# Heads 4 to 7 of the first batch through block transposes and transposing DMAs, a smaller scale for q, and weights asked for later

## The chip, the cores and the metric

The kernel runs on one core of one Trainium2 chip. The metric is the device time of one execution in microseconds, taken as the median of several runs. Before the change it is 331.51 us (three runs, 330.75 to 333.87). TensorE is called PE below, VectorE DVE, ScalarE ACT, GpSimd POOL; SP is the engine that issues most of the DMAs.

## The reference

Attention in which a query sees only the keys of its own hash bucket, followed by a feed-forward layer with a layer norm and a residual. Four batches, eight heads, 768 tokens, head width 64, six hash bits, model width 512, hidden width 2048, all in float32:

```python
q_bits = (q @ proj > 0);  k_bits = (k @ proj > 0)          # 6 bits for each token and head
mask = bucket(q_bits) == bucket(k_bits)
scores = where(mask, q @ k.T / 8, -1e9)
attn = softmax(scores) @ v                                  # for each batch and head
x = heads side by side                                      # (4, 768, 512)
out = x + relu(norm(x) * g_ln @ w_ch1) @ w_ch2
```

## The kernel before

**The mask as a matmul.** For each head the kernel keeps q and k transposed, features on partitions 0 to 63, and beside them, on partitions 64 to 69, the six hash bits as plus or minus 24 (`BIT`). One matmul over 70 partitions then gives the score plus 576 for each bit that agrees and minus 576 for each that does not. The exponential (line 373) subtracts the sum for six agreeing bits, so that every other bucket comes out as zero. These operands lie in `slots`, one buffer for even and one for odd batches.

**Two ways to make the operands.** For batch 0 all eight heads go through PE (`head`, line 572): `transposes` turns q and k of one head with six float32 transposes, the results are copied out of PSUM by DVE (q) and ACT (k), and `casts` narrows them into `slots` on POOL and DVE or ACT. `hash_pair` multiplies two heads by `proj` (sixteen float32 passes in the trace), DVE takes the signs (line 300), and four DVE instructions multiply by 48 and write the bits into `slots` (line 306). For batches 1 to 3 the work is taken from PE in another manner: POOL narrows q and k to bfloat16 (`narrow`), a transposing DMA writes `slots` (`operands`, line 253) and a plain DMA moves the odd token tiles down from partitions 64 to 127 (line 256); DVE transposes 32x32 blocks of the float32 tile (`blocks`, line 239), PE multiplies these by a block-diagonal `proj` (`hashes`, line 265), DVE takes signs and scales (lines 273 and 276), and the bits go to DRAM (line 278) and come back into `slots` by four DMAs, one for a head, in rows of 64 bytes (line 280).

**Order of the first stage.** The kernel works in twelve chunks of 256 query tokens, three for each batch. A chunk has four pairs of heads and three units in each pair. A unit is four score matmuls (line 367), one exponential over 128 x 1024 (line 373) and eight value matmuls (line 395). The first two chunks are interleaved by hand in `first_two` (line 577): 24 units in the order pair 0 of chunk 0, pair 0 of chunk 1, pair 1 of both, pairs 2 and 3 of chunk 0, pairs 2 and 3 of chunk 1. The table `also` says what else is emitted in the step of each unit, and each engine keeps that order. In step i the scores of unit i + 1 are emitted first, then the entries of `also[i]`, then the values of unit i. Heads 4 and 5 (pair 2) are first needed by unit 12, heads 6 and 7 by unit 15. Before the change, `head(4)` to `head(7)` stand in steps 5 to 11 and their bits in steps 8 and 12; the layer norm of chunk 0 stands in step 18, and the first two of its eight up-projections (line 455) in steps 22 and 23. From chunk 2 on, a planner mixes the units with the feed-forward work by costs.

**DMA queues.** SP and ACT issue plain DMAs, each on a queue of its own (q1 and q10 in the profile). The weights are cast from float32 to bfloat16 on the way, and POOL issues those DMAs on a third queue (q0): `load_w1` (line 492) straight after `values(0)`, `load_w2` (line 500) in step 7. Each SP or ACT DMA takes the next of eight semaphores and waits at issue for the DMA that used it last. The inputs of batch 1 (`nxt.load(0)`) are asked for at the start, `nxt.load(1)` and `nxt.load_v(0)` in step 9.

Of the kernel before, what the change touches and what calls it, by code (L numbers as in the profile page):

```python
# [16 lines left out]

BIT = 24.0
LBIT = BIT * BIT

# [6 lines left out]
def kernel(  # L27
# [11 lines left out]
    nc = tc.nc  # L39
# [49 lines left out]
    HS = HC * P  # L89
    CMAP = [[2 * i + par for par in range(2) for i in range(HC)]] + [list(range(NC))] * (B - 1)  # L90
    slots = [
# [41 lines left out]
    def load_half(b, half):  # L133

        first = b == 0
        h0 = half * H // 2
        t = {}
        for nm in "qk":
            t[nm] = nat.tile([P, H // 2, NC, D], F32, tag=f"{nm}nat", name=f"{nm}nat")
        cuts = [0, 1, 2, 4] if first and half == 0 else [0, 2, 4]  # L140
        for lo, hi in zip(cuts, cuts[1:]):
            for nm, src, eng in (
                ("q", q, nc.sync), ("k", k, nc.scalar if first else nc.sync)
            ):
                eng.dma_start(
                    out=t[nm][:, lo:hi],
                    in_=src[b, h0 + lo : h0 + hi].rearrange("h (p c) d -> p h c d", p=P),
                )
            if first and half == 0 and lo == 1:
                for i in range(2):  # L150
                    nc.scalar.dma_start(
                        out=proj1[i * D : (i + 1) * D, i, 0:n_bits], in_=proj
                    )

                nc.scalar.activation(wake2[:, 0:1], wake2[:, 1:2], AF.Exp)
                t["v"] = load_values(b, half)
        return t
# [15 lines left out]
    class Prep:  # L173
# [28 lines left out]
        def transposes(self, h, a):  # L202

            if a == 0:
                self.qkT[h] = work.tile([P, 2, HS], F32, tag="qkT", bufs=4, name="qkT")
            if h == 1:
                tp = ps_sc.tile([P, 2, 512], F32, tag="sc", name="tpose")[:, 0, 0:HS]
            else:
                tp = ps_mm.tile([P, HS], F32, tag="mm", name="tpose")
            for i in range(HC):  # L210
                nc.tensor.transpose(  # L211
                    tp[:, i * P : (i + 1) * P],
                    self.tiles[h // 4]["qk"[a]][:, h % 4, 2 * i : 2 * i + 2].rearrange(
                        "p c d -> p (c d)"
                    ),
                    identf,
                )
            evac(self.qkT[h][:, a, :], tp)

# [8 lines left out]
        def narrow(self, half, a):  # L228

            if a == 0:  # L230
                self.nat16[half] = work.tile(
                    [P, H // 2, 2, NC, D], BF16, tag="nat16", bufs=1, name="nat16"
                )
            nc.gpsimd.tensor_copy(self.nat16[half][:, :, a], self.tiles[half]["qk"[a]])  # L234

# [10 lines left out]

        def operands(self, half):


            dst = self.sl[:, half * H // 2 : (half + 1) * H // 2].rearrange(  # L250
                "p h a (i two t) -> p (h a i) two t", two=2, t=P
            )
            nc.sync.dma_start_transpose(
                out=dst[:, :, 0, :], in_=self.nat16[half].rearrange("p h a c d -> p (h a c d)")
            )
            nc.sync.dma_start(out=dst[0:D, :, 1, :], in_=dst[D:P, :, 0, :])

        def hashes(self, half):
# [16 lines left out]
            )  # L275
            nc.vector.tensor_scalar_mul(bits, bits, 2.0 * BIT)
            bd = bounce.tile([P, 2 * NT_], BF16, tag="bits", name="bits_d")
# [11 lines left out]
        def hash_pair(self, j):  # L289
# [14 lines left out]
            for g in range(4):  # L304
                par = g % 2
                nc.vector.tensor_scalar_mul(  # L306
                    self.sl[D:K1, 2 * j + g // 2, :, par * HS : (par + 1) * HS],
                    bits[32 * g : 32 * g + n_bits],
                    2.0 * BIT,
                )  # L310

# [13 lines left out]
        def part(self, kind, half):  # L325

            if kind == "T":
                return [(0, lambda: self.operands(half))]
            if kind == "H":
# [19 lines left out]
    def att_units(b, t, x):  # L349

        sl, va, vs = slots[b % 2], vaug[b % 2], vsum[b % 2]
        units = []
        q0 = t * CT
        for j in range(NP):
# [7 lines left out]
            for g, grp in enumerate(groups):  # L362

                def scores(grp=grp, g=g, state=state):
                    sc = ps_sc.tile([P, 4, CT], F32, tag="sc", name="sc")
                    for i, (h, kj) in enumerate(grp):
                        nc.tensor.matmul(  # L367
                            sc[:, i, :],
                            sl[0:K1, h, 1, kj * P : (kj + 1) * P],
                            sl[0:K1, h, 0, q0 : q0 + CT],  # L370
                        )
                    ex = work.tile([P, 4, CT], BF16, tag="ex", bufs=3, name="ex")
                    nc.scalar.activation(ex, sc, AF.Exp, bias=expb, scale=scale)  # L373
                    state[g] = ex

                def values(grp=grp, g=g, state=state, j=j, ha=ha):
# [16 lines left out]
                    for i, (h, kj) in enumerate(grp):  # L393
                        for qi in range(TT):
                            nc.tensor.matmul(  # L395
                                av[:, h - ha, qi, :],
                                state[g][:, i, qi * P : (qi + 1) * P],
                                va[:, h, CMAP[b][kj], :],
                                start=False,
                                stop=(g == 2 and i == 3),  # L400
                                skip_group_check=True,
                            )
# [16 lines left out]
    def mlp_steps(b, t, x):  # L419
# [43 lines left out]
        def down(i, part):  # L463
# [8 lines left out]
            if part == 3:  # L472
# [4 lines left out]
                nc.sync.dma_start(  # L477
                    out=out[b].rearrange("(p c) d -> p c d", p=P)[:, CMAP[b][t * TT + i], :],
                    in_=x[:, i, :],
# [97 lines left out]
    def first_two():  # L577
# [4 lines left out]
        prep.load_v(1)  # L582
        nxt.load(0)
        tp = ps_mm.tile([P, P], F32, tag="mm", name="wakep")
        for _ in range(26):
# [4 lines left out]
        prep.values(0)  # L590
        load_w1()
        groups = [(0, 0), (0, 1), (1, 0), (1, 1), (2, 0), (3, 0), (2, 1), (3, 1)]
        seq = [(n, 3 * j + g) for j, n in groups for g in range(3)]

        also = {
            0: [lambda: head(2)],
            2: [lambda: head(3), lambda: prep.values(1)],
            3: [lambda: prep.hash_pair(1)],
            5: [lambda: head(4), lambda: prep.value_sums(1)],
            7: [lambda: head(5), load_w2],  # L600
            8: [lambda: prep.hash_pair(2)],
            9: [lambda: head(6), lambda: nxt.load(1), lambda: nxt.load_v(0)],
            11: [lambda: head(7)],
            12: [lambda: prep.hash_pair(3)],
            14: [block_diagonal, lambda: nxt.narrow(0, 0), lambda: nxt.narrow(0, 1)],
            15: [lambda: nxt.blocks(0, 0, 0), lambda: prep.value_sums(0)],
            16: [lambda: nxt.blocks(0, 0, 1)],
            18: [mlp[0][0][1]],
            20: [lambda: nxt.blocks(0, 1, 0)],
            21: [lambda: nxt.blocks(0, 1, 1), lambda: nxt.operands(0)],  # L610
            22: [mlp[0][1][0][1]],
# [247 lines left out]
```

## Time and profile before

| | |
|---|---|
| median of the runs | 331.51 us (330.75 to 333.87) |
| the profiled execution's own time | 333.12 us |
| its span in the profile | 331.3 us |
| PE busy | 311.1 us, 94% of the span |
| ACT, DVE, POOL busy | 215.4, 163.7 and 87.0 us |
| granted PE clock | 0.964 of full speed, mean |
| start of the exponential of unit 0, 12 and 23, and of the first unit of chunk 2 | 12.74, 32.88, 51.95 and 56.29 us |

Times within the profile count from the start of its span, and the profiled execution is 1.6 us above the median. A line such as "L306 DVE" names the source line and the engine; "idle before, releaser" says what the engine waited for. The granted clock falls to half in two stretches, from about 14 to 17 us and from 41 to 58 us, where a matmul takes about twice as long.

### The profile page before, as it was taken

To read this page: it belongs to the slowest core of one execution; us is meant where nothing else is said; L and a number is where in the kernel's file an instruction comes from. 1 tells how busy PE (TensorE), PEld (TensorE's weight loads), DVE (VectorE), ACT (ScalarE), POOL (GpSimd) and SP (SyncE) were. 2 spreads that over 40 slices of the span, in tenths; PEclk is the share of its full clock that TensorE was granted. 3 is DMA by queue.
4 is the path that set the end of the run, shared out by engine and by line. 5 is a ranking of instruction groups with operands and counts; after the bars stand their busy time and mean duration, and the time that the engine had idled before them with its cause. 6 is when DMAs were issued, how large, how long until landed. Compare 5 with 4: busy or idle time off the path is not lost.

```text
span 331.3 us, 7771 instructions
## 1 busy us (share of the span) xinstructions
PE 311.1 (94%) x3254; PEld 230.7 (70%) x3280; DVE 163.7 (49%) x330; ACT 215.4 (65%) x268; POOL 87.0 (26%) x111
## 2 busy tenths in 40 slices
PE   8799698899989999989999999999999999999992
PEld 6477376766957967857868868858769679687660
DVE  1568993664483393353475464524532633535420
ACT  2577574854585795786895886898758667565110
POOL 2738922853130442055164030010200200200100
PEclk9899955999999999999999999999999999999997
DMA  7999976896469459487633533020020110200301
GB/s 268 372 251 294 273 133 130 184 207 185 134 144 233 100 185 232 103 222 224 134 73 89 99 85 80 2 66 32 2 65 33 32 67 2 63 34 2 96 3 69
DMA packets 68425, 41.45 MB, mean 125 GB/s; under 512 B 49056, under 2 KB 64160, under 8 KB 68384
## 3 DMA queue, kind: packets, MB, share of 16 engines
q1 hardware_dynamic: 63984, 35.12, 41.0%
q0 software_dynamic: 3136, 4.19, 7.1%
q10 hardware_dynamic: 1264, 1.58, 1.3%
q8 instruction: 27, 0.44, 0.5%
q14 instruction: 14, 0.11, 0.1%
HBM read 27.97 MB, written 6.88 MB: 105 GB/s over the span
## 4 chain that ended last, share of the span: by engine, by line
PE 76%; DVE 8%; ACT 6%; issue 4%; DMA 3%; ACTq 0%; DVEq 0%
PE hp L455 25%; PE o L468 21%; PE sc L367 16%; PE av L395 9%; ACT junk L191 3%; DVE slots L306 3%; PE hash L265 3%; ACT ex L373 2%; PE av L386 2%; DMA proj<-in_proj_dram 2%; DVE bits L300 1%; DMA xnT<-xn 1%; DVE stats L430 1%; PE tpose L211 1%; ACT qkT L130 1%
## 5 line engine op out<-in xcount | busy, mean ns | idle before, releaser
L373 ACT ACTIVATE ex<-sc,expb 128x1024 bf16<-128x1024 f32 x144 | 159.5, 1111 | 75.0 <-PE sc L367 74.9
L455 PE MATMUL hp<-xnT,w_sb 128*128 128x256 bf16 x768 | 100.3, 276 | 2.8 <-DVE hbuf L126 1.6
L367 PE MATMUL sc<-slots 70*128 70x256 bf16 x576 | 91.2, 282 | 5.2 <-DVE slots L306 5.1
L468 PE MATMUL o<-w_sb,hbuf 128*128 128x512 bf16 x358 | 94.1, 379 | 1.4
L455 PEld LDWEIGHTS <-w_sb 128*128 128x128 bf16 x768 | 72.7, 98 | 12.7 <-issue 3.3
L395 PEld LDWEIGHTS <-ex 128*128 128x128 bf16 x1152 | 55.8, 100 | 19.4 <-ACT ex L373 7.6
L367 PEld LDWEIGHTS <-slots 70*128 70x128 bf16 x576 | 52.5, 100 | 21.5 <-POOL vaug L314 2.9
L126 DVE TENSOR_SCALAR hbuf<-hp 128x512 bf16<-128x512 f32 x48 | 33.2, 691 | 63.8 <-PE hp L455 63.8
L395 PE MATMUL av<-vaug,ex 128*128 128x65 bf16 x1152 | 61.6, 198 | 2.0 <-ACT ex L373 1.9
L468 PEld LDWEIGHTS <-hbuf 128*128 128x128 bf16 x384 | 35.1, 97 | 27.5
L444 POOL TENSOR_SCALAR rs<-mv 128x2 f32<-128x2 f32 x12 | 6.1, 512 | 167.9 <-DVE mv L431 167.9
L130 ACT ACTIVATE hbuf<-hp 128x512 bf16<-128x512 f32 x48 | 28.5, 593 | 21.5 <-PE hp L455 21.0
L473 DVE SCALAR_TENSOR_TENSOR x<-o,rs,x 128x512 f32<-128x512 f32 x24 | 17.8, 743 | 46.2 <-PE o L468 44.2
L406 DVE TENSOR_TENSOR x<-av,rc 128x256 f32<-128x256 f32 x48 | 20.4, 424 | 1.6
L405 DVE RECIPROCAL rc<-av 128x4 f32<-128x4 f32 x48 | 8.5, 176 | 19.3 <-PE av L395 19.3
L432 DVE SCALAR_TENSOR_TENSOR xn<-x,mv,gbc 128x512 bf16<-128x512 f32 x24 | 17.3, 743 | 0.1
L323 POOL TENSOR_TENSOR vacc<-vacc,vaug 128x256 f32<-128x256 f32 x24 | 16.2, 676 | 1.3
L430 DVE BATCH_NORM_STATS2 stats<-x 128x6 f32<-128x512 f32 x24 | 15.4, 679 | 0.2
L314 POOL CAST vaug<-vnat 128x1536 bf16<-128x1536 f32 x8 | 12.4, 1550 | 9.1 <-PE av L395 5.5
L234 POOL CAST nat<-qnat 128x1536 bf16<-128x1536 f32 x6 | 8.8, 1466 | 20.0 <-DMA out_dram<-x 12.6
L191 ACT ACTIVATE junk<-qnat 128x768 bf16<-128x768 f32 x16 | 13.5, 843 | 0.1
L191 ACT ACTIVATE junk<-knat 128x768 bf16<-128x768 f32 x16 | 13.4, 837 | 0.2
(59 smaller groups left out, 189.2 us busy)
## 6 DMA issues: line engine op xcount, KB each, us to landing
vnat<-in_v_dram SPq DMA_DIRECT2D x8, 768.0 KB
out_dram<-x SPq DMA_DIRECT2D x24, 256.0 KB
qnat<-in_q_dram SPq DMA_DIRECT2D x15, 384.0 KB
knat<-in_k_dram SPq DMA_DIRECT2D x12, 384.0 KB
w_sb<-in_moe_w_ch_dram POOLq DMA_DIRECT2D x4, 1024.0 KB, 15.2
slots<-slots SPq DMA_DIRECT2D x6, 384.0 KB
knat<-in_k_dram ACTq DMA_DIRECT2D x3, 384.0 KB
bits_d<-bits SPq DMA_DIRECT2D x6, 96.0 KB
```

The costliest lines, as they stand in the source:

```text
L126: nc.vector.tensor_scalar_max(dst, src, 0.0)
L130: nc.scalar.activation(dst, src, AF.Relu if relu else AF.Copy)
L191: nc.scalar.activation(junk, self.tiles[half]["qk"[a]][:, 2 * j : 2 * j + 2].rearrange("p h c d -> p (h c d)"), AF.Square, accum_out=sq[:, ...
L367: nc.tensor.matmul(sc[:, i, :], sl[0:K1, h, 1, kj * P : (kj + 1) * P], sl[0:K1, h, 0, q0 : q0 + CT],)
L373: nc.scalar.activation(ex, sc, AF.Exp, bias=expb, scale=scale)
L395: nc.tensor.matmul(av[:, h - ha, qi, :], state[g][:, i, qi * P : (qi + 1) * P], va[:, h, CMAP[b][kj], :], start=False, stop=(g == 2 and i ...
L406: nc.vector.tensor_tensor(x[:, :, ha * D : (ha + 2) * D].rearrange("p t (h d) -> p h t d", h=2), av[:, :, :, 0:D], rc.unsqueeze(3).to_broa ...
L430: nc.vector.bn_stats(stats, x[:, i, :])
L432: nc.vector.scalar_tensor_tensor(xn[:, :, i, :], x[:, i, :].rearrange("p (o d) -> p o d", d=P), mv[:, i, 0:1], gbc.rearrange("p (o d) -> p ...
L455: nc.tensor.matmul(hp[:, i, :], w1_sb[:, dt, nt * P : (nt + 1) * P], st["xnT"][:, dt, :], start=(dt == 0), stop=(dt == ND - 1),)
L468: nc.tensor.matmul(o2, st["h"][:, nt, i * P : (i + 1) * P], w2_sb[:, nt, :], start=(nt == 0), stop=(nt == NH - 1),)
L473: nc.vector.scalar_tensor_tensor(x[:, i, :], o2, st["rs"][:, i : i + 1], x[:, i, :], op0=AOP.mult, op1=AOP.add,)
```

## The change

- **Scale.** q is multiplied by 2^-12 when it leaves PSUM or is narrowed, the bits stay plus or minus one half, and the exponential's scale grows by 2^12. The multiplications of the bits (lines 276 and 306) go. In `hash_pair(0)` the four writes of bits become two DVE copies and two ACT copies; in `hash_pair(1)` they become four DMAs on SP.
- **Heads 4 to 7 of batch 0** take the way of the other batches: q narrowed on DVE, k on POOL, two transposing DMAs of two heads each, the odd tiles moved by two DVE copies, four block transposes on DVE, `hashes(1)` on PE, and the bits through DRAM. Heads 4 to 7 then lie in natural tile order, and the chunks of batch 0 take the tile pairs (0,2), (1,3), (4,5) so that one order serves both halves.
- **DMAs.** Most k loads move from ACT's queue to SP's; v of the first half comes after q and k of it. `load_w1` moves from ahead of the units to step 1, behind the casts of heads 2 and 3; `nxt.load(0)` from the start to step 8, behind `hashes(1)`; `nxt.load(1)` and `nxt.load_v(0)` from step 9 to step 10.

```diff
+Q_SCALE = 2.0**-12
+LBIT = 0.25 / Q_SCALE
+    def tile_order(b, h):
+        return EVEN_FIRST if b == 0 and h < H // 2 else list(range(NC))
+    def query_tiles(b, t):
+        return ((0, 2), (1, 3), (4, 5))[t] if b == 0 else (2 * t, 2 * t + 1)
...
-            for nm, src, eng in (
-                ("q", q, nc.sync), ("k", k, nc.scalar if first else nc.sync)
-            ):
+            for nm, src in (("q", q), ("k", k)):
+                eng = nc.scalar if nm == "k" and hi - lo == 1 else nc.sync
...
-            evac(self.qkT[h][:, a, :], tp)
+            if a == 0:
+                nc.vector.tensor_scalar_mul(self.qkT[h][:, a, :], tp, Q_SCALE)
+            else:
+                nc.scalar.activation(self.qkT[h][:, a, :], tp, AF.Copy)
...
+            if a == 1:
+                nc.gpsimd.tensor_copy(dst, src)
+            elif self.b == 0:
+                nc.vector.tensor_scalar_mul(dst, src, Q_SCALE)
+            else:
+                nc.gpsimd.tensor_scalar_mul(dst, src, Q_SCALE)
...
+        def operands(self, half, lo=0, n=4):
             nc.sync.dma_start_transpose(
+                out=self.pair_places(half * H // 2 + lo, n)[:, :, 0, :],
+                in_=self.nat16[half][:, lo : lo + n].rearrange("p h a c d -> p (h a c d)"),
             )
+        def odd_tiles(self, half, lo=0, n=4):
+            dst = self.pair_places(half * H // 2 + lo, n)
+            if self.b == 0:
+                nc.vector.tensor_copy(dst[0:D, :, 1, :], dst[D:P, :, 0, :])
+            else:
+                nc.sync.dma_start(out=dst[0:D, :, 1, :], in_=dst[D:P, :, 0, :])
...
-            nc.vector.tensor_scalar_mul(bits, bits, 2.0 * BIT)
             bd = bounce.tile([P, 2 * NT_], BF16, tag="bits", name="bits_d")
...
+                if j > 0:
+                    nc.sync.dma_start(out=dst, in_=src)
+                elif g < 2:
+                    nc.vector.tensor_copy(dst, src)
+                else:
+                    nc.scalar.activation(dst, src, AF.Copy)
...
-        nxt.load(0)
...
         prep.values(0)
-        load_w1()
+        prep.narrow(1, 1)
...
-            0: [lambda: head(2)],
-            2: [lambda: head(3), lambda: prep.values(1)],
-            3: [lambda: prep.hash_pair(1)],
-            5: [lambda: head(4), lambda: prep.value_sums(1)],
-            7: [lambda: head(5), load_w2],
-            8: [lambda: prep.hash_pair(2)],
-            9: [lambda: head(6), lambda: nxt.load(1), lambda: nxt.load_v(0)],
-            11: [lambda: head(7)],
-            12: [lambda: prep.hash_pair(3)],
-            14: [block_diagonal, lambda: nxt.narrow(0, 0), lambda: nxt.narrow(0, 1)],
+            0: [
+                lambda: prep.transposes(2, 0), lambda: prep.transposes(2, 1),
+                lambda: prep.narrow(1, 0), lambda: prep.casts(2),
+                lambda: prep.operands(1, 0, 2), lambda: prep.operands(1, 2, 2),
+            ],
+            1: [lambda: head(3), load_w1],
+            3: [lambda: prep.hash_pair(1), block_diagonal, lambda: prep.values(1)],
+            4: [lambda: prep.blocks(1, 0, 0), lambda: prep.blocks(1, 1, 0)],
+            5: [
+                lambda: prep.blocks(1, 0, 1), lambda: prep.blocks(1, 1, 1),
+                lambda: prep.value_sums(1),
+            ],
+            6: [lambda: prep.odd_tiles(1, 0, 2)],
+            7: [lambda: prep.odd_tiles(1, 2, 2), load_w2],
+            8: [lambda: prep.hashes(1), lambda: nxt.load(0)],
+            10: [lambda: nxt.load(1), lambda: nxt.load_v(0)],
+            14: [lambda: nxt.narrow(0, 0), lambda: nxt.narrow(0, 1)],
```

## The prediction

> **What bounds the kernel now.** First the page: PE is busy for 94% of the span, and the chain of work that ended last is 76% PE. From 70 us on PE is busy for 96% of the time, so what the first stage loses or gains is carried to the end. The change touches little outside that stage, so I read the windows there. Columns: length, busy time and count on PE, PE weight loads, DVE, ACT and POOL, then the granted PE clock, the DMA share and GB/s.
>
> ```profile
> 33.00:37.00 4.00, 3.43 (x46) 2.11 (x46) 3.73 (x10) 2.59 (x3) 3.35 (x3) 1.00 1.11 337
> 37.00:41.20 4.20, 1.61 (x24) 0.93 (x21) 4.10 (x4) 2.16 (x2) 3.96 (x6) 0.98 1.23 220
> 41.20:53.00 11.80, 10.62 (x89) 7.44 (x90) 10.29 (x24) 8.91 (x9) 2.65 (x4) 0.50 0.77 131
> 53.00:58.00 5.00, 4.96 (x34) 3.64 (x34) 0.69 (x1) 1.19 (x3) 1.37 (x1) 0.50 0.72 135
> ```
>
> PE works 1.61 of 4.2 us up to 41.2, and then its clock stands at 0.50 until 58, although PE is never idle for long in between. What PE waited for at 37 to 41 is in the chain by time (start, length, what):
>
> ```profile
> 36.89 2.13 DVE slots L306
> 39.05 0.66 DVE slots L306
> 39.74 0.70 DVE slots L306
> 40.45 0.73 DVE slots L306
> 41.23 0.61 PE sc L367 x2
> ...
> 49.63 3.37 DMA xnT<-xn
> 53.04 1.86 PE hp L455 x8
> ```
>
> The bits of heads 6 and 7 come late from DVE, and the first up-projection waits for the layer norm's transpose. The DMA share is above 1 from 8 to 46 us, so transfers also matter. The DMA view of four windows (packets, MB, share of 16 engines) shows who gets what: 18 to 22 us, 43 to 46, 51 to 56, 84 to 86.
>
> ```profile
> q0 software_dynamic: 284, 0.58, 76.5%
> q1 hardware_dynamic: 282, 0.40, 33.1%
> ...
> q0 software_dynamic: 600, 0.61, 123.3%
> ...
> q1 hardware_dynamic: 4095, 1.04, 111.7%
> ...
> q1 hardware_dynamic: 852, 0.06, 29.2%
> ```
>
> From 18 to 22 us w1 (q0) and the inputs (q1) each move the same number of packets: the engines take one from each in turn, whatever its size. A w1 packet occupies an engine for 0.765 x 4 us x 16 / 284 = 172 ns. From 43 to 46 us w2 is alone: 3 us x 16 / 600 = 80 ns a packet. From 51 to 56 us 32 transposed blocks go in 4095 packets, 5 us x 16 / 4095 = 20 ns each. From 84 to 86 us the 64-byte rows of the bits (line 280) use 29% of 16 engines, about five; I take six, one for each bit row: 2 us x 6 / 852 = 14 ns each.
>
> **The change, part by part.** All against the profiled execution (own time 333.1 us, span 331.3); its median is 1.6 us lower.
>
> *Start.* ACT's copy of k of head 0 stood until 7.65 us behind ACT's k loads (issues at 4.10, 5.08 and 7.23); those move to SP. The second hash then follows the first: DVE's second signs start at about 9.3 instead of 10.33. Two of the four bit writes (2.22 us together) go to ACT. I take -1.2 us; bounds -2 and 0 (proj still lands near 7.2 us).
>
> *Pair 1.* head(3) comes a step earlier; its hash ran at 19.31 to 20.8 and should end near 19.7. The four DVE writes (1.93 us) become four small DMAs. No row shows one; the nearest, the bits' way to DRAM, took 2.3 us from issue (71.97) to its reader (74.31). Against 1.93 that is about +1 with the issue, so unit 6 starts about where it did (23.5). Bounds: 0 and +3.
>
> *Work taken from PE.* Heads 4 to 7 lose 24 transposes (four heads at about 0.33 us for three, 2.6 us) and two hashes of 1.50 us; `hashes(1)` adds 1.51 (row at 67.44): 4.1 us less. ACT loses four copies of 0.48. DVE loses eight copies of 0.56, four signs and the slow eight of line 306 (2.58 and 4.29), some 13 us, and gains a narrowing (POOL's took 1.46; 1 to 1.7), four block transposes of 0.96, signs of 0.52 and two copies (0.35 to 2.1 by the spread of line 306): 7 to 10 us. This lets units 6 to 11 run at the exponential's pace (1.11 us) but for the hash and two openings, against 1.6 on average. Unit 11 ends near 31 us instead of 33. All of this pays only if heads 4 to 7 are ready then.
>
> *Transposes.* The narrowed tile is ready near 15 us. Two DMAs of 12 blocks: 24 blocks took 3.71 us to issue and land 5.5 us after it began, so they land near 21. w1's packets began about 4 us after POOL's issue (11.63; the rate falls at 16). POOL now issues after casts(3), near 17, so they begin near 21. It just fits. If 300 packets were left, each would wait for a w1 packet: 300 / 16 x 0.19 = +3.6 us.
>
> *Bits of heads 4 to 7: the step that decides.* DVE has, after pair 1's signs at about 20: the block diagonal (2.1), four block transposes (3.8), a reciprocal with its product (0.6), two copies (1 to 1.5). It is free near 28, as is PE after the scores of unit 9. Hash 1.5 us less the overlap and signs 0.52: bits at 29.1. The two weight transfers need 11 us (w1: 64 packets an engine at 172 ns) and 10 us (w2: 128 at 80 ns), so from 21 us they last past 42 in any case, and now stand beside this chain; before, the same chain ran at 72 us with no weights. To DRAM: 2.3 us, and 16 packets an engine each behind a w1 packet, 16 x 0.19 = 3: 34.5 us. Back: 48 packets an engine for each head, on six engines, one after the other: with w2 in turn 48 x (80 + 14) ns = 4.5 us a head. With 1.3 us before the first packet and as much after the last (estimates from that 2.3), head 4 arrives at 41.5, head 5 at 46; then w2 runs out on those engines and heads 6 and 7 follow at 48 and 48.7.
>
> *Sum.* Unit 12 needs head 4: exponential at 41.5 instead of 32.88. Unit 13 needs head 5: 46 instead of 34.90. PE idles for some 10 us, longer than where its clock fell before, so units 13 to 23 run at the spacing of the half clock (1.45 us, from 42 to 52 us): unit 23 at 46 + 10 x 1.45 = 60.5, against 51.95: +8.5. The norm, its transpose and the two slow ups add 4.3 us as before. I add 0.5 for batch 1's loads, which now wait behind the bits. The start's -1.2 is already in these times. Own time 333.1 + 9 = 342.1; less 1.6, **341 us**.
>
> *Costed at nothing.* Line 276 (0.22 to 1.16 us, six times) lies under PE in later stages. POOL's scaled narrowing there may take 1.5 us or, at the pace of its tensor operations (0.66 us for 256 elements), 4; POOL is busy for 36 of the last 211 us, and the cover is a chunk of some 25 us. `load_w1` later costs nothing until the first up. `nxt.load(0)` is behind the bits on SP's queue: its reader on DVE, the block transposes of steps 15 and 16, has the reciprocals behind it, and lands about 50 us, just in time; uncovered, 1 to 3 us. Strided q columns in the scores have no row; none is expected.
>
> *A page against the trace.* The granted clock stayed at 0.50 from 41.2 to 58 us with PE busy for 10.62 of 11.8. The Trainium skill, "TensorE: Matmul & The Clock Gate" (Part 1), says that one busy window of some 3.4 us brings the full clock back; the trace does not agree while the work is attention units, and the sum goes by the trace. By the page, the second rival below would hold.
>
> **The rivals.**
> 1. *Small packets are let through; the clock holds* (faster). If the engines take several small packets in a turn, the bits need 2.3 us out and about 2.5 back for the first head: unit 12 near 34 to 35, a wait of 3 us. If the clock also holds, units run at 1.2 us and the first chunk-2 exponential comes at about 53 instead of 56.29: -3.5 us, 328. It turns on the engines' turns being larger than one packet, at less than 30 ns a row. Against it: the equal counts at 18 to 22 us, and the clock that fell after 37 to 41. For it: no row has rows of 64 bytes beside weights.
> 2. *The wait is there, the clock recovers*: 10 units save 0.25 us each and two ups 0.9 each, -4.3: 337.
> 3. *The small packets get less than their turn*, so the bits come only when w2 is through (47 us or later), or the transposes run into w1: unit 12 at 47 to 49: +13 to 15, 346.
> 4. *Small packets are let through, but the clock falls*: unit 12 +2, the slower units over again, PE work saved: within 1% of before, 332.
>
> **How the numbers follow.** Forecast 0.45, rival 2 0.10, rival 3 0.20, rival 4 0.10, rival 1 0.15. Faster 0.15, same 0.10, slower 0.75; 1% (3.3 us) is about what a measurement of this kernel can tell from no change. The range runs from 329, which takes in rival 4 and the unknown gains of the start, to 348 (transposes in w1, late bits); some 0.10 is left below and 0.08 above.
>
> **What would show it.** Score matmuls of unit 12 waiting for a DMA of bits for about 10 us; rows of line 280 landing over 10 us beside q0; the clock at 0.5 from the middle of the 30s to about 67 us; the chunk-2 exponential at 64 to 66. Wrong if these rows land within 5 us of their issue, or if q0 has ended by 35 us.

## The result and the profile after

The changed kernel takes **346.99 us** (median of four runs, 344.66 to 349.19) against 332.62 for the kernel before in the same comparison (330.75 to 333.87): a ratio of 1.0436, 95% interval 1.034 to 1.0532. It is slower by 14.4 us where 9.5 were forecast. The profiled execution took 349.19 us, with a span of 347.4, so it is 16.1 us above that of before, and 2.2 above its own median.

First the page of the changed kernel: PE's share, and two groups (busy time, mean ns, idle time before them and what ended most of it).

```profile
PE 308.6 (89%) x3230; PEld 229.4 (66%) x3256; DVE 154.7 (45%) x306; ACT 215.5 (62%) x266; POOL 99.7 (29%) x108
...
L397 PE MATMUL sc<-slots 70*128 70x256 bf16 x576 | 93.3, 287 | 25.2 <-DMA slots<-bits 14.1
...
L251 POOL TENSOR_SCALAR nat<-qnat 128x1536 bf16<-128x1536 f32 x6 | 24.7, 4113 | 59.0 <-DMA qnat<-in_q_dram 39.8
```

PE has 2.5 us less to do than before and still loses 5 points of its share: it waits. The score matmuls (line 397, line 367 before) stood 25.2 us idle, 14.1 of them in one wait for bits. The view of waits from 8 to 75 us (total, times, longest) shows two:

```profile
PE sc L397 <- DMA slots<-bits: 14.1, 1, 14.1
...
PE sc L397 <- DMA slots<-bits_d: 9.6, 1, 9.6
```

`slots<-bits` are the four small DMAs with the bits of heads 2 and 3, `slots<-bits_d` the way back from DRAM for heads 4 to 7. The second wait was forecast, at about 10 us. The first was not. The chain by time (start, length, what) puts them in place:

```profile
16.97 1.16 POOL slots L233
...
20.55 12.82 DMA slots<-bits
...
33.50 1.01 PE sc L397 x4
...
38.56 1.48 PE hash L292 x32
...
40.07 0.56 DVE bits L300
...
40.65 5.28 DMA bits_d<-bits
45.95 6.07 DMA slots<-bits_d
...
52.07 1.04 PE sc L397 x4
```

The windows answer to those shown of before (length, busy time and count on PE, PE weight loads, DVE, ACT and POOL, granted clock, DMA share, GB/s):

```profile
20.00:25.00 5.00, 0.00 (x0) 0.00 (x0) 4.90 (x8) 0.39 (x1) 4.68 (x6) 0.85 1.34 104
25.00:30.00 5.00, 0.00 (x0) 0.00 (x0) 2.16 (x3) 0.00 (x0) 2.42 (x4) 0.50 1.09 116
...
45.00:50.00 5.00, 0.00 (x0) 0.00 (x0) 0.00 (x0) 0.00 (x0) 0.00 (x0) 0.74 0.87 140
...
60.00:65.00 5.00, 5.00 (x48) 3.67 (x48) 2.99 (x7) 3.84 (x4) 4.94 (x3) 0.50 0.97 352
65.00:70.00 5.00, 3.66 (x29) 2.36 (x28) 3.87 (x7) 3.76 (x4) 4.29 (x7) 0.50 0.45 84
```

PE does nothing at all from 20 to 30 and from 45 to 50 us. The DMA engines are full from 20 to 30 us (shares 1.34 and 1.09) and move little (104 and 116 GB/s); from 45 to 50 us their share is 0.87. After the second wait the clock stays at 0.50 until 74 us. The same places in both kernels and in the experiments (start of the exponential of a unit, us, from one profiled execution each):

| kernel | median, us | ratio to before, 95% interval | unit 2 | 6 | 11 | 12 | 23 | chunk 2 |
|---|---|---|---|---|---|---|---|---|
| before | 332.6 | | 17.35 | 23.59 | 31.87 | 32.88 | 51.95 | 56.29 |
| changed | 347.0 | 1.0436, 1.034 to 1.0532 | 14.26 | 34.61 | 42.25 | 53.20 | 69.09 | 73.38 |
| 1, bits of heads 2, 3 by copies | 345.0 | 1.0385, 1.0326 to 1.0443 | 14.06 | 22.72 | 31.91 | 49.20 | 63.98 | 69.70 |
| 2, weights after the bits | 356.9 | 1.0757, 1.0678 to 1.0836 | 13.66 | 23.14 | 32.16 | 36.21 | 52.10 | 74.46 |
| 3, half weight rows | 345.0 | 1.0368, 1.0323 to 1.0413 | 16.69 | 28.78 | 37.49 | 50.40 | 66.29 | 70.60 |
| 4, PE kept busy | 347.8 | 1.045, 1.0373 to 1.0526 | 13.89 | 35.99 | 42.86 | 51.92 | 63.90 | 71.68 |
| 5, heads 4 to 7 by PE | 337.6 | 1.0111, 1.0045 to 1.0176 | 16.37 | 23.69 | 32.59 | 33.59 | 54.28 | 58.26 |
| 6, the same, late loads | 336.1 | 1.0109, 1.0072 to 1.0146 | 14.17 | 21.83 | 31.13 | 32.12 | 52.82 | 56.82 |
| 7, w2 after the bits | 345.4 | 1.0395, 1.0354 to 1.0435 | 14.45 | 21.78 | 29.16 | 41.16 | 56.72 | 65.92 |
| 8, batch 1 first, weights last | 347.2 | 1.0433, 1.0386 to 1.0479 | 15.10 | 22.47 | 30.90 | 35.53 | 51.09 | 65.20 |
| 9, as 6, narrowing on DVE | 335.1 | 1.0067, 1.003 to 1.0104 | 16.44 | 24.11 | 33.41 | 34.41 | 51.98 | 56.49 |
| 10, as 5, narrowing on DVE | 333.2 | 1.0019, 0.9996 to 1.0042 | 15.92 | 23.24 | 32.14 | 33.14 | 51.32 | 55.54 |
| 11, changed, narrowing on DVE | 345.5 | 1.0357, 1.0307 to 1.0408 | – | – | – | – | – | – |
| 12, as 10, half of it | 332.4 | 0.9995, 0.9961 to 1.0028 | 14.96 | 22.29 | 31.20 | 32.19 | 50.23 | 54.23 |

One run of 6 and one of 11 were slow: they count in the medians and not in the ratios, and the profile of 11 is of its slow run, so its places are left out.

### The profile page after: what moved, and what is told of

Read it like the earlier page. It is cut to its first block, busy times and chain, and to the rows that moved or that the text cites. A ratio compares the mean times of both kernels' runs of the same rounds, so it can differ in the third digit from the quotient of the medians.

```text
span 347.4 us, 7688 instructions
## 1 busy us (share of the span) xinstructions
PE 308.6 (89%) x3230; PEld 229.4 (66%) x3256; DVE 154.7 (45%) x306; ACT 215.5 (62%) x266; POOL 99.7 (29%) x108
## 4 chain that ended last, share of the span: by engine, by line
PE 74%; DMA 11%; ACT 5%; issue 4%; DVE 3%; SPq 1%; POOL 0%; ACTq 0%; DVEq 0%; POOLq 0%
PE hp L487 24%; PE o L500 20%; PE sc L397 16%; PE av L427 9%; DMA slots<-bits 4%; ACT junk L199 3%; PE hash L292 3%; DMA qnat<-in_q_dram 2%; DMA slots<-bits_d 2%; PE av L418 2%; ACT ex L405 2%; DMA bits_d<-bits 2%; DMA knat<-in_k_dram 1%; DMA xnT<-xn 1%; DVE xn L464 1%
## 5 line engine op out<-in xcount | busy, mean ns | idle before, releaser
L397 PE MATMUL sc<-slots 70*128 70x256 bf16 x576 | 93.3, 287 | 25.2 <-DMA slots<-bits 14.1
L397 PEld LDWEIGHTS <-slots 70*128 70x128 bf16 x576 | 53.4, 101 | 41.7 <-issue 17.5
L427 PE MATMUL av<-vaug,ex 128*128 128x65 bf16 x1152 | 62.4, 199 | 2.0 <-ACT ex L405 1.9
L500 PEld LDWEIGHTS <-hbuf 128*128 128x128 bf16 x384 | 35.1, 97 | 27.5
L251 POOL TENSOR_SCALAR nat<-qnat 128x1536 bf16<-128x1536 f32 x6 | 24.7, 4113 | 59.0 <-DMA qnat<-in_q_dram 39.8
L464 DVE SCALAR_TENSOR_TENSOR xn<-x,mv,gbc 128x512 bf16<-128x512 f32 x24 | 18.5, 793 | 0.1
```

Source lines behind the costliest of these rows:

```text
L251: nc.gpsimd.tensor_scalar_mul(dst, src, Q_SCALE)
L397: nc.tensor.matmul(sc[:, i, :], sl[0:K1, h, 1, kj * P : (kj + 1) * P], sl[0:K1, h, 0, :].rearrange("p (c t) -> p c t", t=P)[:, lo : hi + 1 ...
L427: nc.tensor.matmul(av[:, h - ha, qi, :], state[g][:, i, qi * P : (qi + 1) * P], va[:, h, tile_order(b, h)[kj], :], start=False, stop=(g == ...
L464: nc.vector.scalar_tensor_tensor(xn[:, :, i, :], x[:, i, :].rearrange("p (o d) -> p o d", d=P), mv[:, i, 0:1], gbc.rearrange("p (o d) -> p ...
L500: nc.tensor.matmul(o2, st["h"][:, nt, i * P : (i + 1) * P], w2_sb[:, nt, :], start=(nt == 0), stop=(nt == NH - 1),)
```

## The experiments

The theory after this result: both waits come from small packets that take turns with the weights on the DMA engines. The transposes of heads 4 to 7 were not through when w1 began, and the bits of heads 2 and 3 stand behind them on SP's queue.

**1. Bits of heads 2 and 3 by copies.**

```diff
-                if j > 0:
-                    nc.sync.dma_start(out=dst, in_=src)
-                elif g < 2:
+                if g < 2:
                     nc.vector.tensor_copy(dst, src)
```

> The changed kernel, but the bits of heads 2 and 3 are written by DVE and ACT copies again instead of four DMAs. Turns (one packet of q1, then one weight packet): the wait of 14.2 us before unit 6 goes, since only the DMAs of the bits stood behind the transposes; unit 6 starts near 21 to 22 us. The last transposed tiles still land near 31 us, so DVE's odd tiles and the signs end near 33 (40.6 in the changed kernel) and unit 12 starts near 46 instead of 53.2: about 341 us. Issue order on SP (the DMAs are late because SP hands them out one behind the other, weights or not): the same first gain, and the bits of heads 4 to 7 take as long from their signs to unit 12 as before, 12.6 us. Clock (the loss is mostly the half clock): under 3 us gained, 345 us or more.

Unit 6 is back at 22.72 us, so the first wait came with these four DMAs. The total fell by 2 us only, to 345.0 where turns gave 341, and its interval overlaps that of the changed kernel: the second wait grew, and unit 12 came at 49.20, not near 46. Its chain:

```profile
18.60 13.69 DMA slots<-nat
...
33.36 5.95 DMA bits_d<-bits
...
39.33 8.70 DMA slots<-bits_d
...
48.07 1.04 PE sc L395 x4
```

`slots<-nat` are the transposes: they take 13.69 us. The DMA view of this kernel (packets, MB, share of 16 engines) shows why, for 18 to 21.4 us, before w1's packets come, and for 21.4 to 32.4:

```profile
q1 hardware_dynamic: 2272, 0.57, 93.8%
q0 software_dynamic: 1, 0.00, 0.3%
...
DMA packets 1589, 1.69 MB, mean 153 GB/s; under 512 B 876, under 2 KB 876, under 8 KB 1588
...
q0 software_dynamic: 635, 1.28, 84.7%
```

2272 packets of the transposes went in 3.4 us alone; the last 876 small ones took 11 us beside 635 of w1. Over these 11 us a w1 packet takes an engine 0.847 x 11 x 16 / 635 = 235 ns, against 172 in the kernel before. But this is a mean of two states. Of the 876, 288 went by 22.0 us beside 13 of w1. The same view for 22 to 25 us and for 28 to 31:

```profile
q0 software_dynamic: 91, 0.19, 93.9%
q1 hardware_dynamic: 145, 0.04, 51.6%
...
q0 software_dynamic: 252, 0.50, 90.5%
q1 hardware_dynamic: 249, 0.08, 19.2%
```

From 28 to 31 us the two queues go one to one (in what turns the counts don't tell), and a w1 packet takes 0.905 x 3 x 16 / 252 = 172 ns, as before. From 22 to 25 us, though, it takes 495 ns, and so few packets of either queue move. So turns are one part of the delay, and the slow first packets of w1 another; why these are slow is open. When the transposes land (32.3 us), the odd tiles on DVE and with them the hash's signs and the bits come late.

**2. Weights only after the bits.** Both weights are asked for behind a small POOL copy that reads the bits of head 7.

```diff
-            1: [lambda: head(3), load_w1],
+            1: [lambda: head(3)],
...
-            7: [lambda: prep.odd_tiles(1, 2, 2), load_w2],
-            8: [lambda: prep.hashes(1), lambda: nxt.load(0)],
+            7: [lambda: prep.odd_tiles(1, 2, 2)],
+            8: [lambda: prep.hashes(1), after_bits, load_w1, load_w2, lambda: nxt.load(0)],
```

> The changed kernel, but both weights are asked for only when the bits of head 7 have landed (a small POOL copy of those bits into the first weight tile, which the weight DMA then overwrites, makes POOL wait). Turns: nothing stands beside the transposes and the bits, so the transposes land near 21 to 22 us, unit 6 starts near 23 to 25, the chain from the signs of heads 4 to 7 to unit 12 takes 5 to 6 us instead of 12.6, and unit 12 starts near 34 to 36. The weights then land after 50 us, and the first up-projection waits for w1 until about 55: near 333 us, 331 to 338. Issue order on SP: unit 6 not before 30 us, unit 12 not before 45, and the late weights come on top: 350 us or more.

Its chain:

```profile
19.58 2.33 DMA slots<-bits
...
30.57 1.63 DMA bits_d<-bits
...
32.22 2.82 DMA slots<-bits_d
...
50.08 21.08 DMA xnT<-xn
```

With no weights beside them the same DMAs take 2.33 instead of 12.82, 1.63 instead of 5.28 and 2.82 instead of 6.07 us, and unit 12 comes at 36.21. So the weights beside them make both waits, and the order on SP's queue alone does not. The total is nevertheless the worst, 356.9: the layer norm's transposing DMA now goes beside the weights, behind the loads of batch 1 on its queue, and takes 21.08 us where it took 3.37 before. My total for this kernel missed that; experiments 7 and 8 return to it.

**3. Weight rows halved.** The loads move the same bytes in twice as many rows of half the size.

```diff
-        for cs in range(0, hidden, hidden // 2):
+        for cs in range(0, hidden, hidden // 4):
```

(and the same for `w2_sb`, whose rows are cut to 256 columns)

> The changed kernel, with the rows of both weights cut in half: twice as many weight packets of half the size, the same bytes. Turns: a q1 packet waits half as long, so the tail of the transposes and the bits of heads 2 and 3 land near 27 to 28 us instead of 33.4, unit 12 starts near 46 to 48 instead of 53.2: about 341 us. Shared bytes (the engines divide their time by bytes or the weights simply fill them) or issue order on SP: no change, 345 to 349 us.

It does not test the size of a turn cleanly, because the start came out otherwise: the transposes were issued at 16.36 us instead of 17.05, w1's packets began about 22, and all 3123 packets up to 21.5 us were SP's. So the transposes were through, the bits of heads 2 and 3 took 6.73 instead of 12.82 us, and unit 6 came at 28.78. The bits of heads 4 to 7 gained nothing: 5.28 us out again, and 8.03 back. Halving the packets did not halve their delay; from 42 to 46 us 1416 packets of w2 went beside 385 of the bits. The total, 345.0, is the figure of the rivals and not the 341 that shorter turns gave. The DMA view of the changed kernel, whose bits are sent out at 40.65 us, says more, for 41 to 44 us, where SP's queue (q1) has no line at all, and for 44.1 to 45.9:

```profile
q0 software_dynamic: 599, 0.61, 122.5%
...
q0 software_dynamic: 278, 0.28, 92.5%
q1 hardware_dynamic: 144, 0.10, 22.6%
```

No packet of the bits moves for some 3.5 us, and then all 144 go within 1.8. With the halved rows it is the same: sent out at 35.90, none by 39.5 us, while 1345 packets of the weights pass from 36 us on. With a turn for each packet some of them would have gone from the start. So what the weights delay on this way is the first packet, not each one, and what holds it is open. The other thing that this kernel shows is that a start 0.7 us earlier decides whether the transposes run into w1.

**4. PE kept busy in both waits**, with 220 and 150 matmuls on constants behind units 4 and 10, so that the clock does not fall.

> The changed kernel, with 220 small matmuls of the warm-up kind put in step 4 and 150 in step 10, where PE otherwise idles for 14 and 10 us; their results are not used. Turns: the two waits stay, unit 6 near 34 us and unit 12 near 53. Clock: if the half clock after the waits costs what the spacing of the units says (about 17 units at 1.45 instead of 1.2 us, two up-projections at 1.86 instead of 0.88), the time falls by 4 to 6 us, to about 342, and the granted clock stays at 1.0 through both. If units are paced by something else, the time stays within 2 us of 347.

Windows of this kernel, as above:

```profile
45.00:50.00 5.00, 5.00 (x93) 5.00 (x91) 0.00 (x0) 0.00 (x0) 0.00 (x0) 1.00 0.64 104
50.00:55.00 5.00, 4.34 (x70) 3.36 (x67) 0.61 (x2) 3.07 (x3) 0.00 (x0) 1.00 0.85 253
55.00:60.00 5.00, 4.20 (x61) 2.92 (x62) 2.82 (x6) 4.97 (x6) 1.23 (x1) 1.00 1.03 371
```

The clock stays at 1.00 through the second wait (the first 220 matmuls did not last through the first one: 0.82 from 35 to 40 us), and units 12 to 20 follow one another at 1.07 us instead of 1.41. Nothing is gained in the total (347.8, where 342 was expected), and its chain tells why:

```profile
51.07 7.55 DMA qnat<-in_q_dram
58.64 0.98 DVE bt L256
...
64.99 3.40 DMA xnT<-xn
```

q of batch 1, asked for behind the bits, lands at 58.6. DVE's block transposes wait for it, and the layer norm of chunk 0 stands behind them on DVE. The half clock of the changed kernel lies beside this wait.

**5. Heads 4 to 7 through PE again**, heads and loads at their places of before. The scale of q, the k loads on SP and the bits by plain copies stay.

```diff
-        return EVEN_FIRST if b == 0 and h < H // 2 else list(range(NC))
+        return EVEN_FIRST if b == 0 else list(range(NC))
...
-        prep.narrow(1, 1)
+        load_w1()
...
+            5: [lambda: head(4), lambda: prep.value_sums(1)],
+            7: [lambda: head(5), load_w2],
+            8: [lambda: prep.hash_pair(2)],
+            9: [lambda: head(6), lambda: nxt.load(1), lambda: nxt.load_v(0)],
+            11: [lambda: head(7)],
+            12: [lambda: prep.hash_pair(3)],
```

> Heads 4 to 7 of batch 0 go through PE again, heads and loads stand where they stood before, and the scale of q, the bits by plain copies (two on DVE, two on ACT) and the k loads on SP stay. If the loss lies in the way of heads 4 to 7 and in the order of the loads: no score waits for a DMA after the first inputs, unit 2 starts near 14.3 us as in the changed kernel (17.35 before), unit 12 near 31 (32.88 before), chunk 2 near 54 to 55, total 329 to 331 us, a little faster than the kernel before. Rival: the scale itself costs (POOL's scaled narrowing took 4.11 us for each of six instead of 1.46, the query tiles of the scores lie apart): then PE or DVE waits show in later chunks and the total is 335 us or more.

337.6 us: 9.4 less than the changed kernel, so most of the loss lies in what is taken back here: the way of heads 4 to 7, the bits of heads 2 and 3 by DMAs, and the late loads, which 6 puts back. But it is 1.1% slower than the kernel before, as the rival said. Unit 15, which needs the bits of heads 6 and 7, came at 42.87 instead of 40.15. The timelines of POOL and DVE in this kernel (start, length, engine, line, what, count):

```profile
36.45 4.12 POOL L251 TENSOR_SCALAR nat<-qnat 128x1536 bf16<-128x1536 f32 x1
...
29.49 1.08 DVE L335 COPY slots<-bits 6x768 bf16<-6x768 bf16 x2
...
37.19 5.13 DVE L335 COPY slots<-bits 6x768 bf16<-6x768 bf16 x2
```

The same two copies took 1.08 us at 29.49, and 5.13 at 37.19, beside POOL's scaled narrowing of q, which is itself 4.12 us long where the plain cast took 1.46.

**6. The same with the loads as late as in the changed kernel.**

```diff
+            2: [lambda: head(3), load_w1, lambda: prep.values(1)],
+            7: [lambda: head(5), load_w2],
+            8: [lambda: prep.hash_pair(2), lambda: nxt.load(0)],
+            10: [lambda: nxt.load(1), lambda: nxt.load_v(0)],
```

> As the kernel with heads 4 to 7 by PE, but with the loads as late as in the changed kernel: w1 behind the casts of head 3, the first loads of batch 1 in step 8, the others in step 10. Theory (late loads of batch 1 are a cost of their own, beside the late bits): unit 12 near 31 us, then DVE's block transposes wait for q of batch 1 until 50 to 56 us, the layer norm stands behind them, first up-projection 55 to 60 us instead of 53, total 333 to 338 us. Rival (only the bits' way through the queues costs): as the kernel with early loads, 329 to 331 us.

336.1 us, in the range of the theory but not for its reason: the profiled run has the same 4.1 us of POOL in front of unit 15 (41.40), and the kernel's interval lies within that of experiment 5. The profile is of its fastest run (333.0). Late loads cost nothing that these two can tell.

**7. w1 after the transposes, w2 after the bits, batch 1 at the start**, with the heads by DMA as in the changed kernel and the bits of heads 2 and 3 by copies.

```diff
+        nxt.load(0)
...
+            3: [lambda: prep.hash_pair(1), block_diagonal, lambda: prep.values(1), after_transposes, load_w1],
...
+            8: [lambda: prep.hashes(1), lambda: after_bits(w2_sb), load_w2],
```

> The changed kernel with the bits of heads 2 and 3 by copies, the first loads of batch 1 asked for at the start, w1 asked for once the transposes of heads 4 to 7 have landed and w2 once the bits of head 7 have. Theory (each transfer of small packets loses only what stands beside it): transposes land by 24 us, unit 6 near 23, bits out beside w1 take some 5 us and back some 3, unit 12 at 36 to 40 us; w2 is through by 50, the layer norm's transpose takes about 4 us, first up-projection 55 to 58, total 333 to 338 us. Rival (the way of heads 4 to 7 is too late whatever the order of the loads, or the loads of batch 1 now push the transposes back): unit 12 at 45 or later, total 343 or more.

**8. As 2, but the first loads of batch 1 at the start**, the others behind the layer norm:

```diff
+        nxt.load(0)
...
+            8: [lambda: prep.hashes(1), lambda: after_bits(w1_sb), load_w1, load_w2],
...
+            18: [mlp[0][0][1], lambda: nxt.load(1), lambda: nxt.load_v(0)],
```

> As the kernel with both weights asked for after the bits of head 7 and with the bits of heads 2 and 3 by copies, but the first loads of batch 1 are asked for at the start and the others behind the layer norm of chunk 0. It tells what made that kernel slow (357 us): theory, the loads of batch 1 ahead of the layer norm's transpose on SP's queue: unit 12 near 36 us, the transpose goes beside w1 and w2 alone in 5 to 10 us, first up-projection 57 to 62, total 336 to 342 us. Rival, the weights themselves are then too late: first up-projection still near 70 us, total 350 or more.

Chain of 7, then of 8:

```profile
28.97 6.28 DMA bits_d<-bits
35.30 4.62 DMA slots<-bits_d
...
54.61 8.01 DMA xnT<-xn
```

```profile
29.83 1.63 DMA bits_d<-bits
31.51 2.77 DMA slots<-bits_d
...
49.31 12.59 DMA xnT<-xn
...
86.74 6.68 DMA xnT<-xn
```

Neither comes near the kernel before (345.4 and 347.2), and both totals are above what the theory gave. In 7 the bits go beside w1 and unit 12 waits until 41.16; then the norm's transpose goes beside w2 for 8.01 us. In 8 the bits are quick and unit 12 comes at 35.53, but the transposes of chunk 0 and of chunk 1 take 12.59 and 6.68 us. The loads of batch 1 were only part of what made experiment 2 slow (the transpose went from 21.08 to 12.59); the weights beside it are the rest. Each order moves the wait to another transfer of small packets.

**9 and 10. q of batch 1 narrowed on DVE** instead of POOL, in the kernels of 6 and 5; **11** the same in the changed kernel.

```diff
-            elif self.b == 0:
+            elif self.b <= 1:
                 nc.vector.tensor_scalar_mul(dst, src, Q_SCALE)
```

> As the kernel with heads 4 to 7 by PE and late loads, but q of batch 1 is narrowed with its scale on DVE instead of POOL (0.96 us on DVE in the changed kernel, against 4.12 on POOL). Theory (POOL's scaled narrowing holds up DVE's copies of bits that run beside it: two took 5.13 us there against 1.08 without it): these copies take 1.1 to 2 us, unit 15 comes at 38 to 39 us instead of 41.4, chunk 2 at 53 to 55, total 332 to 334 us, level with the kernel before or a little faster. Rival (the copies are slow for another reason, such as the engines' memory traffic from the loads): the copies still take 4 to 5 us and the total stays near 336.

> As the kernel with heads 4 to 7 by PE and early loads, but q of batch 1 is narrowed with its scale on DVE. Theory (POOL's scaled narrowing is what made that kernel slower than the one before): unit 15 at 39 to 40 us instead of 42.9, the stretch from chunk 2 to chunk 3 back from 35.7 to 33 us, total 331 to 334 us. Rival (k loads on SP beside the early loads of batch 1 cost more than the scale): unit 2 stays at 16.4 us and the total above 335.

> The changed kernel with the one edit that q of batch 1 is narrowed with its scale on DVE. It tells how much of the changed kernel's loss is POOL's scaled narrowing. Theory (there it lies behind the late loads of batch 1, and only the layer norm's subtraction of 1.20 us stands beside it): 0 to 2 us less, 345 to 347. Rival (it is a main part of the loss): 342 or less.

DVE in kernel 10, at the place shown for 5:

```profile
36.74 1.49 DVE L335 COPY slots<-bits 6x768 bf16<-6x768 bf16 x2
...
41.17 0.96 DVE L249 TENSOR_SCALAR nat<-qnat 128x1536 bf16<-128x1536 f32 x1
```

The copies take 1.49 us instead of 5.13, unit 15 comes at 39.47 instead of 42.87, and the total falls from 337.6 to 333.2 (0.9% by the ratios), level with the kernel before. So POOL's narrowing made kernel 5 slow. With late loads (9) the same edit gives less, 336.1 to 335.1, above the range I gave, with intervals that overlap, and 9 stays 0.7% slower than before. In the changed kernel (11) it gives 1.5 us by the medians and 0.8% (2.6 us) by the ratios, and these intervals overlap too: there POOL's narrowing stands behind the late loads. One expectation failed in 10: the stretch from chunk 2 to chunk 3 stayed at 35.1 us (32.8 before).

**12. Only the first half of batch 1 by DVE**, the second by POOL, otherwise as 10.

```diff
-            elif self.b == 0:
+            elif self.b == 0 or (self.b, half) == (1, 0):
```

> As the kernel with heads 4 to 7 by PE, early loads and q of batch 1 narrowed on DVE, but only the first half of batch 1 goes by DVE, the second by POOL as in the changed kernel. In the former, DVE's narrowing of the second half stood at 59.20 us between the statistics and the subtraction of chunk 1's layer norm, PE was idle from about 59.6 to 62.3 us and its clock then fell to 0.5 until about 67. Theory (that idle time makes the stretch from chunk 2 to chunk 3 35 us long instead of 32.8): chunk 2 near 55.5 us, the stretch 32 to 33 us, total 331 to 332 us, a little under the kernel before. Rival (the stretch is long because POOL's scaled narrowing then stands beside the layer norm, as it was with 35.7 us in the kernel with early loads and POOL's narrowing): the stretch 35 us, total 333 to 335.

332.4 us, ratio 0.9995 (0.9961 to 1.0028): no difference to the kernel before. Against 5 it has this one edit and is 5.2 us quicker (1.2% by the ratios). The stretch from chunk 2 to chunk 3, though, is 35.6 us here too, where I gave 32 to 33: DVE's narrowing between the norm's instructions was not its only cause, and with POOL's in its place the rival's figure came. The windows show PE idle for 2.85 of the 4 us from 58 to 62, and a clock that falls behind it:

```profile
58.00:60.00 2.00, 0.74 (x13) 0.60 (x11) 2.00 (x5) 2.00 (x5) 1.94 (x2) 1.00 0.43 102
60.00:62.00 2.00, 0.41 (x4) 0.37 (x4) 1.53 (x2) 1.56 (x5) 1.85 (x3) 1.00 0.56 170
62.00:64.00 2.00, 2.00 (x15) 1.56 (x14) 0.69 (x1) 0.77 (x1) 1.92 (x4) 0.70 1.17 216
64.00:66.00 2.00, 2.00 (x18) 1.48 (x16) 0.00 (x0) 0.94 (x2) 1.84 (x3) 0.50 1.02 160
```

PE is idle there in every kernel, waiting for the layer norm of chunk 1 and the evictions behind it. In the profiled runs of before and of kernel 6 it is idle for 1.6 of 4 us (60 to 64) and the clock holds; in those of 5, 9, 10 and 12 for 2.7 to 3.0, and it falls to 0.50 for some 3 us. Which of DVE's and POOL's instructions makes the idle time longer is open; each profile is one execution.

**Where the 14.4 us are**, by the ratios: from the kernel before to 10, 0.6 us; from 10 to 9, loads as late as in the changed kernel, 1.6; from 9 to 11, heads 4 to 7 and the bits of heads 2 and 3 through the DMAs, 9.6; from 11 to the changed kernel, the narrowing on POOL, 2.6. The first, second and fourth are near what a measurement can tell, with intervals that overlap; the third is not.

## Why the prediction was right, and where it was wrong

The direction and the second wait were right, and 347 lies in the range. The forecast itself, 341, took the wrong case of two: rival 3, with the transposes running into w1 and 346 us, is what happened. It is what experiment 1 shows alone, with unit 12 at 49.20 (rival 3 had 47 to 49); in the changed kernel unit 12 came at 53.20, since the bits of heads 2 and 3 stood behind the same transposes, which no rival had. That the total is near 346 all the same is partly luck: the units behind unit 12 were quicker than in the sum.

- ***Start.*** -0.96 us at unit 0 in the profiled run, -1.2 taken. Right, though the kernels with the same start spread from 11.2 to 12.7 us at that place.
- ***Pair 1.*** With no weights about, the price was right: the four DMAs took 2.33 us (experiment 2) and unit 6 came at 23.14, against 23.5 forecast. The sum left out that they stand behind the transposes on SP's queue. When those met w1 they took 12.82 us, and unit 6 came 11.0 us later than before, where the bounds were 0 and +3.
- ***Transposes: "it just fits".*** This is the step that failed. The narrowed tile was complete at 17.0 us, not 15: DVE's narrowing waited for q until 14.14, and POOL's of k ran from 15.21 to 17.03. w1's packets came at 21.4, as forecast (21). So packets were left and not none: 876 small ones after 21.4 us, counted in experiment 1. The price that I had put beside it (each waits for one w1 packet, 0.19 us) gives 876 / 16 x 0.19 = 10.4 us for them, and 10.9 passed, from 21.4 to 32.3. That these agree is luck: 288 of them went in the first 0.6 us beside 13 of w1, and the others took longer turns, since a w1 packet took 495 ns from 22 to 25 us. The term was mis-sized by its count and by the length of a turn, at the one place where the step had no margin.
- ***Work taken from PE.*** PE's busy time fell by 2.5 us with some matmuls at the half clock, 4.1 were worked out. Unit 11 was to end near 31 us instead of 33, and did not: in experiment 1, where the first wait is gone, its exponential starts at 31.91 us, as before (31.87). Units 6 to 11 follow one another at 1.84 us on the mean there, at 1.65 before; the longest step, 3.5 us, lies between units 9 and 10, where the matmuls of `hashes(1)` wait for DVE's block transposes. The sum did not hang on this, because unit 12 waits for the bits.
- ***Bits of heads 4 to 7.*** The signs ended at 40.6 us, not 29.1, because unit 6 and with it `hashes(1)` had waited. From there the times held: 5.28 us out (5.4 forecast), the last release of unit 12 at 52.0, 11.4 us after the signs (12.4 forecast). The mechanism did not, so the times are luck: I let 16 packets on each engine wait for a w1 packet each; 144 went, 144 / 16 = nine an engine, beside w2, and 3.5 us passed before the first of them moved. The heads did not arrive one after another, 4.5 us apart: unit 13 followed unit 12 by 1.3 us.
- ***Sum.*** Unit 12 came 11.7 us later than forecast, units 12 to 23 took 15.9 us instead of 19.0, since the bits of heads 5 to 7 were there; the units ran at 1.46 us (1.45 forecast), and 4.29 us lay between unit 23 and chunk 2 (4.3). Together chunk 2 came 17.1 us later than before. The term for the half clock, rightly sized, was worth nothing by itself: experiment 4 takes it away, and the late loads of batch 1 hold the end.
- ***Costed at nothing.*** POOL's scaled narrowing took the upper of my two bounds, 4.11 us. In the changed kernel its cover held, but for some 2.6 us that the intervals do not tell from nothing. `nxt.load(0)` was to land near 50, "uncovered, 1 to 3 us"; its block transposes began at 58.39, and in experiment 4 they are the next in line. The strided q columns cost nothing: at the full clock a score matmul of heads 4 to 7 took 272 ns in experiment 4 (52.5 to 64 us), 273 before (70 to 100 us).
- ***Rival 2 and the page.*** The clock stood at 0.50 from 48 to 74 us in the changed kernel with PE busy, as the profile counts it, for 5.00 of 5 us from 55 to 60 and again from 60 to 65. The Trainium skill, "TensorE: Matmul & The Clock Gate" (Part 1), lets one busy window of about 3.4 us bring it back; this trace disagrees as the one before did. Rival 2 was therefore rightly put low.
- ***Rivals 1 and 4*** needed rows that pass quickly beside weights. They are out: 5.28 us beside w2, 1.63 without.

## What to carry to other kernels

Work that moves from an engine to small-packet DMAs must be priced by what else is in the DMA queues at that moment, ahead of it on its own queue too, and by the packets that are still left when a bulk load begins, not by the transfer alone: here the same three transfers took 1.6 to 2.8 us alone and 5 to 13 with the weights about. Where a step "just fits", price the miss as well as the hit. And when a wait is removed, look at once for the next transfer that meets the same bulk load; in four orders of the loads (the changed kernel and experiments 2, 7 and 8) there always was one, and only PE, which needs no DMA for these heads, avoided it.

## What the runs showed of the hardware

- SP's queue, mostly the transposes' 256-byte packets, and the casting w1 load went one to one in experiment 1 once w1 was at its pace: 186 and 184 packets from 25 to 28 us, 249 and 252 from 28 to 31, with 172 ns for a w1 packet in the latter. Equal counts fit turns of several packets as well as of one.
- The first packets of w1 took longer there, 495 ns from 22 to 25 us. They did so with nothing beside them as well: in experiment 7, 51 packets took 65.1% of 16 engines from 26 to 28 us, 408 ns each. In the kernel before, where w1 began beside the input loads, they took 172 ns from the start. Why is open.
- A small DMA that was sent out beside the weights did not move a packet for 3.5 us (144 packets, changed kernel) and for 3.6 us (the same, halved weight rows); with no weights the first went 0.9 us after the issue (experiment 2).
- POOL's multiplication of 128 x 1536 from float32 to bfloat16 took 4.11 us, its cast 1.46, and DVE did the multiplication in 0.96. DVE's plain copies beside the former waited for all of it: one copy took 3.60 us, until 0.2 us after POOL's end. A plain cast does the same: in the kernel before, the first write of bits took 2.13 us from 36.89, until 0.2 us after the end of two casts (35.94 to 38.81). The Trainium skill, "SBUF — State Buffer" (SBUF: two separate sides), describes this as an exclusive lock on a port pair that DVE and GpSimd share, held for a whole instruction; the trace agrees. DVE's 32x32 transposes were not held: two took 1.83 us at 58.39 in the changed kernel, beside a narrowing that began at 58.72.
- Extra matmuls held the clock at 1.00 through a wait of 10 us and through the units after it (experiment 4), where the units alone did not bring it back in 22 us (52 to 74).
